# Five query buffers, three value buffers asked for at a step's end, and the second batch's raw keys behind the queries in SP's queue

## The chip, the cores and the metric

The program runs on one core of a Trainium2 chip. Its time is the device time of one execution in microseconds (us). A profiled execution gives, beside its time, a trace of what each engine did: TensorE (PE: matrix products, transposes), VectorE (DVE), ScalarE (ACT), GpSimd (POOL), and SyncE (SP), which here issues nearly all DMA transfers. Each engine takes its instructions in a fixed order and stands still when the next one has to wait.

## What is computed

Attention that keeps the 32 largest scores of each row, over 8 batches, 8 heads, 576 positions and 64 values per head; its output, 512 values for each of 4608 tokens, goes through a gated network of width 1536.

```python
scores = scale * np.matmul(q, k.transpose(0, 1, 3, 2))
kth = np.partition(scores, -top_k, axis=-1)[..., -top_k:-top_k + 1]
scores = np.where(scores >= kth, scores, -1000000000.0)
attn = np.exp(scores - np.max(scores, axis=-1, keepdims=True))
attn = attn / (np.sum(attn, axis=-1, keepdims=True) + 1e-09)
x = np.matmul(attn, v)            # heads side by side: 4608 x 512
gate = 1.0 / (1.0 + np.exp(-(x @ w_gate)))
out = (gate * (x @ w_val)) @ w_out
```

## The kernel before

**Tiling.** Attention goes in steps. A step is one tile of queries (128 positions, the fifth tile of a batch 64) of one pair of heads; a batch has 5 tiles and 4 pairs, so 20 steps. The steps stand in groups: for batch 0 the tiles 0 to 1, 2 to 3 and 4; for each later batch two groups. Within a group the pairs run outside and the tiles inside. Group 3 is the first of batch 1, so `kraw_3_1_2` is the raw key of the second batch, pair 1, head 2, while `u_0_1_0` belongs to batch 0, tile 1, pair 0.

**One step.** TensorE forms the scores, ScalarE copies them to SBUF (`s`). VectorE finds the top values of eight segments and of what they leave (`cand`, `tops`, `leads`). GpSimd makes the exponent's bias `st` (L344), ScalarE the signs `under` (L348), GpSimd the product `u` (L354), ScalarE the exponentials `e` (L285), VectorE the threshold and the masked `e` (L364, L290). TensorE transposes `e` (L376), ScalarE copies that to `et`, and TensorE weighs the values `v` with it. The output is kept as two parts, `xh` and `xl`, whose sum is the value.

**Keys, queries and values.** Batch 0 takes its keys and queries as they are. From batch 1 on a raw key (`kraw`, 128 x 576) is loaded by SP (L190), copied by ScalarE into the rounded key `k` (L192), and GpSimd subtracts the copy from the raw key in two halves of 288 columns (L194), which leaves the remainder in the lower 64 rows. Raw queries (`qraw`) are treated in the same way. The raw keys of batch 1 have a pool of their own, `bkr`, of one buffer, since the larger pool of the later batches takes memory that the splitting of the weights still holds; queries `qh` have three buffers (`bq`), values two (`bv`).

**Weights.** In the head of the program 18 weight tiles are split: SP loads `wraw` (two buffers, two transfers each), ScalarE, VectorE and TensorE (three products into `wrest`) make a high and a low part `w_split` (L150 to L171), and SP writes it to DRAM (`ws`, L172). The first network units take some of them from SBUF; all later ones are loaded back by SP (`w`, L459, 1 MB each, four buffers).

**The gated network.** Each unit of tokens (three of 256, then of 384) is a list of tasks: `wide` (`pz`, L473 to L475: twelve products for each of two outputs), ScalarE, VectorE and GpSimd for the gate, and `narrow` (L494 to L496). Tasks are put among the steps by milestones.

**What sets the order.** The main loop calls for step n the loads of keys two steps ahead (`fetch`), the value load if step n is the last tile of its pair in its group (`get_values`, L570), the query loads four steps ahead (`ask`) and the scores two steps ahead (`begin`); then the selection of step n, the masking of step n-1, weight splits or network tasks, and transposes and weighing of step n-2. From the end of the splitting on, the three look one step further. These calls are not the order of execution: a scheduler takes the instructions with their dependences and buffers and sets a fixed order for each engine and for SP's queue. `tc.issue_after(x)` in the code makes the scheduler place an instruction behind x. A load into a buffer that is still read waits in SP's queue, and what stands behind it waits too.

Of the kernel before, what the change touches and what calls it, by code (L numbers as in the profile page):

```python
# [30 lines left out]
def tile_topk_attention_then_gated_ffn(  # L31
# [10 lines left out]
    nc = tc.nc  # L42
# [33 lines left out]
    bi = ctx.enter_context(tc.tile_pool(name="bi", bufs=3))  # L76
    b2 = ctx.enter_context(tc.tile_pool(name="b2", bufs=2))
    bk = ctx.enter_context(tc.tile_pool(name="bk", bufs=2 * NP))
    bv = ctx.enter_context(tc.tile_pool(name="bv", bufs=2))
    b1 = ctx.enter_context(tc.tile_pool(name="b1", bufs=1))  # L80
    bs = ctx.enter_context(tc.tile_pool(name="bs", bufs=4))
    bq = ctx.enter_context(tc.tile_pool(name="bq", bufs=3))
    bqr = ctx.enter_context(tc.tile_pool(name="bqr", bufs=2))
    bkr = ctx.enter_context(tc.tile_pool(name="bkr", bufs=1))
    bx = ctx.enter_context(tc.tile_pool(name="bx", bufs=2 * NP))
    b3 = ctx.enter_context(tc.tile_pool(name="b3", bufs=3))
    dram = ctx.enter_context(tc.tile_pool(name="dram", bufs=1, space=bass.MemoryType.DRAM))
# [18 lines left out]

    w_split = [dram.tile([P, 2, 2, NP * P], F32, tag=f"ws{i}", name=f"ws{i}") for i in range(n_w)]

    pools, fresh, copies, ahead = {"first": bkr}, {}, [], []

    def ffn_pools():
        for name, bufs in (("w", 4), ("f2", 3), ("f4", NE), ("fg", FG + 1)):
# [68 lines left out]
    def load_keys(b, p, nm, plain):  # L181

        if plain:
            kt = bk.tile([P, S], F32R, tag="k", name=f"k_{nm}").bitcast(F32)
            (nc.sync if p else nc.scalar).dma_start(kt, k1[p])
            return [kt]
        ks = []
        for h in (2 * p, 2 * p + 1):
            raw = pools["kraw" if b > 1 else "first"].tile([P, S], F32, tag="kraw", name=f"kraw_{nm}_{h}")
            nc.sync.dma_start(raw, k[b, h])  # L190
            kt = bk.tile([P, S], F32R, tag="k", name=f"k_{nm}_{h}")
            nc.scalar.activation(kt, raw, AF.Copy)  # L192
            for part in (slice(0, HALF), slice(HALF, S)):
                nc.gpsimd.tensor_tensor(kt[D:, part], raw[D:, part], kt[D:, part], op=ALU.subtract)  # L194
            ks.append(kt)
        return ks

    def load_values(b, p, nm):
        vt = bv.tile([P, 11, D], F32, tag="v", name=f"v_{nm}")
        nc.sync.dma_start(vt, v[b, p].rearrange("p (c d) -> p c d", d=D))  # L200
        return vt

    def load_queries(b, i, p, plain):
        if plain:
            qt = bq.tile([P, 2 * P], F32R, tag="qh", name=f"qh_{b}_{i}_{p}").bitcast(F32)[:, :P]
            nc.sync.dma_start(qt, q1[i, p])
            return (qt,)
        raw = bqr.tile([P, 2 * P], F32, tag="qraw", name=f"qraw_{b}_{i}_{p}")
        nc.sync.dma_start(raw, q[b, i, p])
        qh, ql = [x.tile([P, 2 * P], F32R, tag=t, name=f"{t}_{b}_{i}_{p}") for x, t in ((bq, "qh"), (pools["ql"], "ql"))]  # L210
        nc.scalar.activation(qh, raw, AF.Copy)
        nc.gpsimd.tensor_tensor(ql, raw, qh, op=ALU.subtract)
        return qh, ql
# [301 lines left out]
    def run(general):  # L515
        steps = [(g, p, i) for g, (_, first, end) in enumerate(groups) for p in range(NP) for i in range(first, end)]
# [3 lines left out]
        def fetch(m):  # L520
            if m < len(steps) and steps[m][2] == groups[steps[m][0]][1]:
                g, p, _ = steps[m]
                b, first, _ = groups[g]
                if first == 0:
                    keys[b, p] = load_keys(b, p, f"{mark}{g}_{p}", not b and not general)

        def get_values(m):
            if steps[m][2] == groups[steps[m][0]][2] - 1:
                g, p, _ = steps[m]
                values[g, p] = load_values(groups[g][0], p, f"{mark}{g}_{p}")  # L530

        def begin(m):
            if m < len(steps):
                g, p, i = steps[m]
                staged[m] = scores(qs.pop(m), keys[groups[g][0], p], i, f"{mark}{groups[g][0]}_{i}_{p}")

        def ask(m):
            if m < len(steps):
                g, p, i = steps[m]
                qs[m] = load_queries(groups[g][0], i, p, not groups[g][0] and not general)  # L540
# [14 lines left out]
        fetched, asked, begun = FETCH, ASK, AHEAD  # L555
# [5 lines left out]
        for n in range(len(steps) + 2):  # L561
            if n < len(steps):
                g, p, i = steps[n]
                b, first, end = groups[g]
                m = n
                further = 1 if "spare" in pools else 0
                for m in range(fetched, n + FETCH + further + 1):
                    fetch(m)
                fetched = n + FETCH + further + 1
                get_values(n)  # L570
                for m in range(asked, n + ASK + further + 1):
                    ask(m)
                asked = n + ASK + further + 1
                for m in range(begun, n + AHEAD + further + 1):
                    begin(m)
                begun = n + AHEAD + further + 1
                J = 2 if i < NT else 1
                nm = f"{mark}{b}_{i}_{p}"
                if general:
                    parts[n] = select_any(J, staged.pop(n), nm)  # L580
                else:
                    parts[n] = select(J, staged.pop(n), col, nm)
                next(parts[n])
                col += J
# [18 lines left out]
            else:  # L603
# [5 lines left out]
                while todo and work < goal:  # L609
                    work += todo.pop(0)()  # L610
            if n < 2:
                continue
            g, p, i = steps[n - 2]
            b, first, end = groups[g]
# [24 lines left out]
            if p == NP - 1 and i == end - 1:  # L639
                while ready < len(units) and sum(units[ready]) <= b * S + min(end * P, S):  # L640
                    tasks = ffn(f"{mark}{ready}", [xs[ready, d] for d in range(NP)], *units[ready], orders[ready > 0], ready > 0)
                    kept = todo[-NE:] if ready > 1 and len(todo) >= NE else []
                    todo[len(todo) - len(kept) :] = tasks[: len(kept) > 0] + kept
                    todo += tasks[len(kept) > 0 :]
                    ready += 1
        for task in todo:
            task()

    run(False)


# [14 lines left out]
    with tc.If(again > 0):  # L666
        run(True)
# [54 lines left out]
```

## Time and profile before

| | |
|---|---|
| median of 3 runs | 1572.98 us (1570.57 to 1573.68) |
| profiled execution | 1572.65 us |
| its span in the trace | 1570.8 us |
| TensorE busy | 1515.2 us, 96% of the span |
| VectorE, ScalarE, GpSimd busy | 1286.7, 1115.9, 1067.2 us (82, 71, 68%) |
| moved by DMA | 344.14 MB, 219 GB/s on average |

The span runs from the first to the last record of the trace; the execution's own time is 1.85 us longer. The share of an engine is an average over stages: a row of forty equal slices shows where in the span an engine is idle. For a stretch of interest the trace can be asked for each engine's busy time, and for the instructions of one engine in order of time, each with the idle time ahead of it and what ended that. In such a row "x2" means that two instructions of the kind followed one another, and the duration is that of both.

### The profile page before, as it was taken

Reading aid. Unit: us, or ns where it says so; the run is one execution under the profiler, and the core shown is the slowest. Engines: PE = TensorE matmul, PEld = TensorE weight load, DVE = VectorE, ACT = ScalarE, POOL = GpSimd, SP = SyncE. Lnnn points to the kernel's source line nnn. Section 1 sums busy time; section 2 is a strip of 40 time slices with the busy share of each in tenths; the row PEclk is TensorE's granted clock in tenths of the full one; section 3 lists DMA queues with packets and bytes.
Section 4 is the critical chain, followed back from the end, with each engine's and each line's share of the span. In section 5 each row is a group of like instructions: output and inputs, shape, how many; then the busy total and the mean of one; then the engine's idle time right before and its main releaser. Section 6 shows DMA issues by size and latency. Waiting matters only on the chain. (4 is left out here: it accounts for less than half of the span.)

```text
span 1570.8 us, 33848 instructions
## 1 busy us (share of the span) xinstructions
PE 1515.2 (96%) x10586; PEld 1382.7 (88%) x10586; DVE 1286.7 (82%) x5806; ACT 1115.9 (71%) x2405; POOL 1067.2 (68%) x1756
## 2 busy tenths in 40 slices
PE   5779899999999999999999999999999999999998
PEld 2347689999999999899999999999999999999998
DVE  7899959999988789888988888987898888888311
ACT  8899867778776677786777667777777777667221
POOL 4566847798766877687666876687766886676211
PEclk9889999999999999999999999999999999999999
DMA  7664588787655765556655666565565575564574
GB/s 250 228 244 146 204 324 306 278 288 278 230 208 177 246 219 199 200 207 216 209 199 180 218 232 217 178 235 202 200 217 184 198 244 195 189 213 176 195 275 159
DMA packets 88894, 344.14 MB, mean 219 GB/s; under 512 B 9856, under 2 KB 36992, under 8 KB 57984
## 3 DMA queue, kind: packets, MB, share of 16 engines
q1 hardware_dynamic: 88560, 341.58, 62.5%
q8 instruction: 86, 1.41, 0.4%
q14 instruction: 104, 0.85, 0.2%
q10 hardware_dynamic: 144, 0.29, 0.1%
HBM read 313.52 MB, written 28.31 MB: 218 GB/s over the span
## 5 line engine op out<-in xcount | busy, mean ns | idle before, releaser
L354 POOL TENSOR_TENSOR u<-s,under 128x288 f32<-128x288 f32 x576 | 458.5, 818 | 141.7 <-ACT under L348 130.7
L336 DVE MAX8 cand<-s 128x8 f32<-128x72 f32 x2304 | 345.8, 217 | 66.6 <-ACT s L244 56.1
L473 PE MATMUL pz<-xh,w 128*128 128x384 f32 (+1 forms) x1184 | 391.4, 333 | 1.0 <-DVE acc L500 1.0
L475 PE MATMUL pz<-xh,w 128*128 128x384 f32 (+1 forms) x1184 | 391.3, 331 | 0.0
L474 PE MATMUL pz<-xl,w 128*128 128x384 f32 (+1 forms) x1184 | 390.2, 330 | 0.3 <-POOL xl L446 0.3
L290 DVE SCALAR_TENSOR_TENSOR e<-s,kths,e 128x576 f32<-128x576 f32 x288 | 281.9, 981 | 0.6 <-ACT e L285 0.3
L348 ACT ACTIVATE under<-s,leads 128x576 bf16<-128x576 f32 x288 | 223.0, 776 | 79.9 <-DVE leads L340 34.4
L364 DVE MAX8 kths<-u 128x8 f32<-128x584 f32 x288 | 219.3, 761 | 46.3 <-POOL u L355 44.6
L285 ACT ACTIVATE e<-s,st 128x576 f32<-128x576 f32 x288 | 209.8, 773 | 63.5 <-POOL st L344 62.9
L481 POOL TENSOR_TENSOR gl<-gf,gh 128x384 fp32r<-128x384 f32 (+1 forms) x156 | 153.7, 986 | 113.4 <-ACT gh L480 109.6
L473 PEld LDWEIGHTS pz<-xh,w 128*128 128x128 f32 x1184 | 223.1, 189 | 2.0 <-DVE acc L500 1.3
L474 PEld LDWEIGHTS pz<-xl,w 128*128 128x128 f32 x1184 | 223.5, 189 | 0.8 <-POOL xl L446 0.6
L475 PEld LDWEIGHTS pz<-xh,w 128*128 128x128 f32 x1184 | 223.4, 189 | 0.1
L377 ACT ACTIVATE et<-pt 128x384 f32<-128x384 f32 x384 | 178.6, 488 | 36.8 <-PE pt L376 35.1
L494 PE MATMUL po<-gh,w 128*128 128x384 f32 (+1 forms) x592 | 195.1, 334 | 1.7 <-DVE acc L500 1.6
L495 PE MATMUL po<-gl,w 128*128 128x384 f32 (+1 forms) x592 | 195.5, 331 | 0.5 <-POOL gl L481 0.5
L496 PE MATMUL po<-gh,w 128*128 128x384 f32 (+1 forms) x592 | 194.8, 330 | 0.0
L376 PE MATMUL pt<-ident,e 128*128 128x128 f32 x1152 | 180.8, 275 | 12.6 <-DVE e L290 9.2
L244 ACT ACTIVATE s<-pss 128x576 f32<-128x576 f32 x252 | 161.0, 639 | 40.3 <-PE pss L237 39.8
L376 PEld LDWEIGHTS pt<-ident,e 128*128 128x128 f32 x1152 | 141.0, 141 | 31.3 <-DVE e L290 9.2
L237 PE MATMUL pss<-k,qh 128*128 128x288 f32 (+2 forms) x588 | 165.2, 299 | 0.7 <-ACT s L244 0.7
L237 PE MATMUL pss<-k,ql 128*128 128x288 f32 (+2 forms) x588 | 160.3, 295 | 0.0
(108 smaller groups left out, 2911.1 us busy)
## 6 DMA issues: line engine op xcount, KB each, us to landing
w<-ws SPq DMA_DIRECT2D x222, 1024.0 KB, 5.0
v<-in_v_dram SPq DMA_DIRECT2D x68, 352.0 KB, 3.3
wraw<-in_w_dram SPq DMA_DIRECT2D x36, 512.0 KB, 4.9
ws<-w_split SPq DMA_DIRECT2D x18, 1024.0 KB, 4.5
qraw<-in_q_dram SPq DMA_DIRECT2D x140, 128.0 KB, 2.9
kraw<-in_k_dram SPq DMA_DIRECT2D x56, 288.0 KB, 3.6
out_dram<-acc SPq DMA_DIRECT2D x40, 192.0 KB, 4.7
out_dram<-acc SPq DMA_DIRECT2D x12, 128.0 KB, 6.5
```

The source lines that it names most:

```text
L237: nc.tensor.matmul(ps[:, half, o : o + n], x[:, h * P : (h + 1) * P], ks[h][:, k0 : k0 + n], start=t == 0, stop=t == len(todo) - 1,)
L285: nc.scalar.activation(e[:, j], s[:, j], AF.Exp, bias=st[:, j : j + 1], scale=1.0 / SHRINK)
L290: nc.vector.scalar_tensor_tensor(e[:, j], s[:, j], kth[j], e[:, j], op0=ALU.is_ge, op1=ALU.mult, accum_out=st[:, 4 + j : 5 + j])
L336: nc.vector.max(cand[:, j, 8 * g : 8 * g + 8], s[:, j, g * SEG : (g + 1) * SEG])
L348: nc.scalar.activation(under[:, j], s[:, j], AF.Sign, bias=bound, scale=-CUT, accum_out=sums[:, j : j + 1])
L354: nc.gpsimd.tensor_tensor(u[:, j, part], s[:, j, part], under[:, j, part], op=ALU.mult)
L364: nc.vector.max(kths[:, n_tiles - col - j : n_tiles - col - j + 8], u[:, j])
L376: nc.tensor.transpose(pt[:, c], ef[:, k0 : k0 + P], ident)
L473: nc.tensor.matmul(ps, wt[:, u, 0, d], xh, start=d == 0, stop=False)
L474: nc.tensor.matmul(ps, wt[:, u, 0, d], xl, start=False, stop=False)
L475: nc.tensor.matmul(ps, wt[:, u, 1, d], xh, start=False, stop=d == NP - 1)
L495: nc.tensor.matmul(ps, wt[:, e % 2, 0, f], gl, start=False, stop=False)
```

## The change

Three pools get more buffers: values 2 to 3, queries 3 to 5, raw keys of batch 1 from 1 to 2. Each query load is entered in a list, `requests`. A raw-key load of batch 1 must stand in SP's queue behind the query load that was entered last when `load_keys` ran. And `get_values(n)`, which stood ahead of the query loads of step n, is called when step n's other work has been written down.

```diff
--- before.py
+++ after.py
@@ -76,12 +76,12 @@
     bi = ctx.enter_context(tc.tile_pool(name="bi", bufs=3))
     b2 = ctx.enter_context(tc.tile_pool(name="b2", bufs=2))
     bk = ctx.enter_context(tc.tile_pool(name="bk", bufs=2 * NP))
-    bv = ctx.enter_context(tc.tile_pool(name="bv", bufs=2))
+    bv = ctx.enter_context(tc.tile_pool(name="bv", bufs=3))
     b1 = ctx.enter_context(tc.tile_pool(name="b1", bufs=1))
     bs = ctx.enter_context(tc.tile_pool(name="bs", bufs=4))
-    bq = ctx.enter_context(tc.tile_pool(name="bq", bufs=3))
+    bq = ctx.enter_context(tc.tile_pool(name="bq", bufs=5))
     bqr = ctx.enter_context(tc.tile_pool(name="bqr", bufs=2))
-    bkr = ctx.enter_context(tc.tile_pool(name="bkr", bufs=1))
+    bkr = ctx.enter_context(tc.tile_pool(name="bkr", bufs=2))
     bx = ctx.enter_context(tc.tile_pool(name="bx", bufs=2 * NP))
     b3 = ctx.enter_context(tc.tile_pool(name="b3", bufs=3))
     dram = ctx.enter_context(tc.tile_pool(name="dram", bufs=1, space=bass.MemoryType.DRAM))
@@ -106,7 +106,7 @@
     w_split = [dram.tile([P, 2, 2, NP * P], F32, tag=f"ws{i}", name=f"ws{i}") for i in range(n_w)]
-    pools, fresh, copies, ahead = {"first": bkr}, {}, [], []
+    pools, fresh, copies, ahead, requests = {"first": bkr}, {}, [], [], []
     def ffn_pools():
         for name, bufs in (("w", 4), ("f2", 3), ("f4", NE), ("fg", FG + 1)):
@@ -185,9 +185,11 @@
             (nc.sync if p else nc.scalar).dma_start(kt, k1[p])
             return [kt]
         ks = []
+        asked = requests[-1].ins
         for h in (2 * p, 2 * p + 1):
             raw = pools["kraw" if b > 1 else "first"].tile([P, S], F32, tag="kraw", name=f"kraw_{nm}_{h}")
-            nc.sync.dma_start(raw, k[b, h])
+            with tc.issue_after(asked) if b == 1 else ExitStack():
+                nc.sync.dma_start(raw, k[b, h])
             kt = bk.tile([P, S], F32R, tag="k", name=f"k_{nm}_{h}")
             nc.scalar.activation(kt, raw, AF.Copy)
             for part in (slice(0, HALF), slice(HALF, S)):
@@ -203,10 +205,10 @@
     def load_queries(b, i, p, plain):
         if plain:
             qt = bq.tile([P, 2 * P], F32R, tag="qh", name=f"qh_{b}_{i}_{p}").bitcast(F32)[:, :P]
-            nc.sync.dma_start(qt, q1[i, p])
+            requests.append(nc.sync.dma_start(qt, q1[i, p]))
             return (qt,)
         raw = bqr.tile([P, 2 * P], F32, tag="qraw", name=f"qraw_{b}_{i}_{p}")
-        nc.sync.dma_start(raw, q[b, i, p])
+        requests.append(nc.sync.dma_start(raw, q[b, i, p]))
         qh, ql = [x.tile([P, 2 * P], F32R, tag=t, name=f"{t}_{b}_{i}_{p}") for x, t in ((bq, "qh"), (pools["ql"], "ql"))]
         nc.scalar.activation(qh, raw, AF.Copy)
         nc.gpsimd.tensor_tensor(ql, raw, qh, op=ALU.subtract)
@@ -567,7 +569,6 @@
                 for m in range(fetched, n + FETCH + further + 1):
                     fetch(m)
                 fetched = n + FETCH + further + 1
-                get_values(n)
                 for m in range(asked, n + ASK + further + 1):
                     ask(m)
                 asked = n + ASK + further + 1
@@ -609,6 +610,7 @@
                 while todo and work < goal:
                     work += todo.pop(0)()
             if n < 2:
+                get_values(n)
                 continue
             g, p, i = steps[n - 2]
             b, first, end = groups[g]
@@ -643,6 +645,8 @@
                     todo[len(todo) - len(kept) :] = tasks[: len(kept) > 0] + kept
                     todo += tasks[len(kept) > 0 :]
                     ready += 1
+            if n < len(steps):
+                get_values(n)
         for task in todo:
             task()
```

The scheduler makes of it another order on SP and GpSimd, and, where keys are converted, on ScalarE. Three places show it. Names end in a running number; `<-` stands ahead of what is read.

**First place: SP's queue in the first part of the splitting**, where weights 3, 12 and 13 are loaded (`wraw`) and the split tiles written (`ws`). Before:

```order
L190 DMA kraw_3_0_1_2651<-in_k_dram 128x576
L206 DMA qh_0_1_2_282<-in_q1_dram 128x128
L135 DMA wraw_3_452<-in_w_dram 128x1024 x2
L190 DMA kraw_3_1_2_2828<-in_k_dram 128x576
L206 DMA qh_0_0_3_378<-in_q1_dram 128x128
L172 DMA ws1_124<-w_split_1_344 128x2048
L190 DMA kraw_3_1_3_2834<-in_k_dram 128x576
L135 DMA wraw_12_555<-in_w_dram 128x1024 x2
L172 DMA ws2_125<-w_split_2_364 128x2048
L206 DMA qh_0_1_3_481<-in_q1_dram 128x128
L135 DMA wraw_13_676<-in_w_dram 128x1024 x2
L190 DMA kraw_3_2_4_3093<-in_k_dram 128x576
```

After:

```order
L192 DMA kraw_3_0_0_2645<-in_k_dram 128x576
L192 DMA kraw_3_0_1_2651<-in_k_dram 128x576
L208 DMA qh_0_0_3_378<-in_q1_dram 128x128
L135 DMA wraw_2_363<-in_w_dram 128x1024 x2
L172 DMA ws0_123<-w_split_0_260 128x2048
L208 DMA qh_0_1_3_479<-in_q1_dram 128x128
L135 DMA wraw_3_452<-in_w_dram 128x1024 x2
L172 DMA ws1_124<-w_split_1_342 128x2048
L135 DMA wraw_12_553<-in_w_dram 128x1024 x2
L208 DMA qh_0_2_0_613<-in_q1_dram 128x128
L172 DMA ws2_125<-w_split_2_362 128x2048
L135 DMA wraw_13_676<-in_w_dram 128x1024 x2
```

Two raw keys now stand together ahead of weight 2, behind raw queries of batch 1, and the keys `kraw_3_1_2`, `kraw_3_1_3` and `kraw_3_2_4` have left the places between weights 3, 12 and 13; the queries `qh` stand further ahead.

**Second place: SP's queue at the end of the splitting**, from the last split tile that is written (`ws17`) through the first reloads of split weights (`w`). Before:

```order
L172 DMA ws17_140<-w_split_17_2261 128x2048
L209 DMA qraw_1_0_1_2659<-in_q_dram 128x256
L209 DMA qraw_1_1_1_2746<-in_q_dram 128x256
L459 DMA w_0_3_2417<-ws3_126 128x2048
L459 DMA w_0_12_2452<-ws12_135 128x2048
L459 DMA w_0_13_2484<-ws13_136 128x2048
L459 DMA w_1_0_2893<-ws0_123 128x2048
L200 DMA v_2_1_2657<-in_v_dram 128x704
L209 DMA qraw_1_0_2_2842<-in_q_dram 128x256
L209 DMA qraw_1_1_2_2959<-in_q_dram 128x256
L459 DMA w_1_1_3027<-ws1_124 128x2048
```

After:

```order
L172 DMA ws17_140<-w_split_17_2259 128x2048
L211 DMA qraw_1_0_1_2657<-in_q_dram 128x256
L211 DMA qraw_1_1_1_2744<-in_q_dram 128x256
L192 DMA kraw_3_1_2_2828<-in_k_dram 128x576
L192 DMA kraw_3_1_3_2834<-in_k_dram 128x576
L461 DMA w_0_3_2415<-ws3_126 128x2048
L461 DMA w_0_12_2450<-ws12_135 128x2048
L461 DMA w_0_13_2482<-ws13_136 128x2048
L461 DMA w_1_0_2891<-ws0_123 128x2048
L202 DMA v_2_2_2826<-in_v_dram 128x704
L211 DMA qraw_1_0_2_2840<-in_q_dram 128x256
L211 DMA qraw_1_1_2_2959<-in_q_dram 128x256
```

The four raw keys from `kraw_3_2_4` on, which stood before `ws17`, and the two of pair 1 are now behind the raw queries of batch 1: two here, ahead of the reload `w_0_3`, the other four behind the twelve rows shown.

**Third place: GpSimd's order around the second tile's `u`** (`u_0_1_0`), at the start of batch 0. Before:

```order
L355 TENSOR_TENSOR u_0_0_0_222<-wanted_110,sums_0_0_0_220 128x2x8
L194 TENSOR_TENSOR k_3_0_0_2647<-kraw_3_0_0_2645,k_3_0_0_2647 64x288 x2
L344 TENSOR_SCALAR st_0_1_0_295<-tops_0_1_0_294 128x2
L354 TENSOR_TENSOR u_0_1_0_298<-s_0_1_0_195,under_0_1_0_299 128x288 x2
L293 TENSOR_SCALAR st_0_0_0_219<-st_0_0_0_219 128x2
L354 TENSOR_TENSOR u_0_1_0_298<-s_0_1_0_195,under_0_1_0_299 128x288 x2
L355 TENSOR_TENSOR u_0_1_0_298<-wanted_110,sums_0_1_0_296 128x2x8
L296 COPY inv_0_0_0_342<-st_0_0_0_219 128x128
L194 TENSOR_TENSOR k_3_0_1_2653<-kraw_3_0_1_2651,k_3_0_1_2653 64x288 x2
L344 TENSOR_SCALAR st_0_0_1_391<-tops_0_0_1_390 128x2
L293 TENSOR_SCALAR st_0_1_0_295<-st_0_1_0_295 128x2
L194 TENSOR_TENSOR k_3_1_2_2830<-kraw_3_1_2_2828,k_3_1_2_2830 64x288 x2
```

After:

```order
L357 TENSOR_TENSOR u_0_0_0_222<-wanted_110,sums_0_0_0_220 128x2x8
L346 TENSOR_SCALAR st_0_1_0_293<-tops_0_1_0_292 128x2
L196 TENSOR_TENSOR k_3_0_0_2647<-kraw_3_0_0_2645,k_3_0_0_2647 64x288 x2
L196 TENSOR_TENSOR k_3_0_1_2653<-kraw_3_0_1_2651,k_3_0_1_2653 64x288 x2
L356 TENSOR_TENSOR u_0_1_0_296<-s_0_1_0_195,under_0_1_0_297 128x288 x2
L295 TENSOR_SCALAR st_0_0_0_219<-st_0_0_0_219 128x2
L298 COPY inv_0_0_0_340<-st_0_0_0_219 128x128
L356 TENSOR_TENSOR u_0_1_0_296<-s_0_1_0_195,under_0_1_0_297 128x288 x2
L357 TENSOR_TENSOR u_0_1_0_296<-wanted_110,sums_0_1_0_294 128x2x8
L346 TENSOR_SCALAR st_0_0_1_391<-tops_0_0_1_390 128x2
L295 TENSOR_SCALAR st_0_1_0_293<-st_0_1_0_293 128x2
```

The halves of the second key, `k_3_0_1`, have moved ahead of both parts of `u_0_1_0`; those of `k_3_1_2` have left this place.

## Rows read from the trace of the kernel before

**Rows 1.** The page: engines' busy time (share, instructions); TensorE's tenths in forty slices.

```profile
PE 1515.2 (96%) x10586; PEld 1382.7 (88%) x10586; DVE 1286.7 (82%) x5806; ACT 1115.9 (71%) x2405; POOL 1067.2 (68%) x1756
...
PE   5779899999999999999999999999999999999998
```

**Rows 2.** Windows: stretch, length, engines' busy us (instructions), granted clock, DMA share, GB/s.

```profile
0.00:40.00 40.00, 23.99 (x86) 11.75 (x88) 30.69 (x135) 32.36 (x52) 19.32 (x38) 0.95 0.71 245
40.00:80.00 40.00, 28.38 (x123) 14.66 (x119) 34.26 (x142) 33.86 (x59) 21.08 (x31) 0.84 0.69 237
80.00:120.00 40.00, 30.78 (x140) 17.11 (x139) 37.96 (x149) 36.70 (x66) 25.50 (x33) 0.83 0.69 243
160.00:200.00 40.00, 35.08 (x199) 25.12 (x199) 36.42 (x121) 35.44 (x70) 34.04 (x46) 0.91 0.61 206
230.00:240.00 10.00, 10.00 (x98) 9.80 (x97) 7.92 (x44) 7.59 (x17) 5.42 (x11) 1.00 0.99 402
```

**Rows 3.** Timeline of SP: start, us, line, transfer [idle before <-what ended it].

```profile
32.18 0.33 SPq L190 DMA_DIRECT2D kraw<-in_k_dram  x1
...
40.19 0.33 SPq L190 DMA_DIRECT2D kraw<-in_k_dram  x1
40.57 1.54 SPq L135 DMA_DIRECT2D wraw<-in_w_dram  x2
```

**Rows 4.** Timeline of GpSimd around 40 us.

```profile
36.76 3.40 POOL L194 TENSOR_TENSOR k<-kraw,k 64x288 fp32r<-64x288 f32 x2 [0.94 <-POOL st L293]
...
41.05 0.22 POOL L344 TENSOR_SCALAR st<-tops 128x2 f32<-128x2 f32 x1
```

**Rows 5.** Timeline of VectorE: the frac of a weight.

```profile
36.53 1.20 DVE L162 SCALAR_TENSOR_TENSOR wt_frac<-wraw 128x1024 fp32r<-128x1024 uint32 x1
```

**Rows 6.** Timeline of ScalarE ahead of the first hole.

```profile
41.30 1.44 ACT L285 ACTIVATE e<-s,st 128x576 f32<-128x576 f32 x2 [0.98 <-POOL st L344]
...
43.13 0.68 ACT L192 ACTIVATE k<-kraw 128x576 fp32r<-128x576 f32 x1 [0.39 <-DMA kraw<-in_k_dram]
...
48.88 1.34 ACT L152 ACTIVATE minus_zero<-wraw 128x1024 f16<-128x1024 f32 x1 [2.07 <-DMA wraw<-in_w_dram]
```

**Rows 7.** Timeline of TensorE: the first hole, and the network's first matmul.

```profile
53.38 1.90 PE L376 MATMUL pt<-ident,e 128*128 128x128 f32 x6 [6.29 <-DVE e L290]
...
107.67 0.68 PE L473 MATMUL pz<-xh,w_split 128*128 128x256 f32 x1
```

**Rows 8.** Timeline of ScalarE ahead of the second hole.

```profile
186.88 0.78 ACT L348 ACTIVATE under<-s,leads 128x576 bf16<-128x576 f32 x1 [2.69 <-POOL u L354]
...
189.59 0.69 ACT L192 ACTIVATE k<-kraw 128x576 fp32r<-128x576 f32 x1
...
191.47 1.10 ACT L171 ACTIVATE w_split<-wrest 128x512 fp32r<-128x512 f32 x2
```

**Rows 9.** Timeline of GpSimd ahead of the second hole.

```profile
179.06 0.79 POOL L194 TENSOR_TENSOR k<-kraw,k 64x288 fp32r<-64x288 f32 x1
...
180.63 1.65 POOL L194 TENSOR_TENSOR k<-kraw,k 64x288 fp32r<-64x288 f32 x1
...
184.44 2.40 POOL L354 TENSOR_TENSOR u<-s,under 128x288 f32<-128x288 f32 x2
```

**Rows 10.** Timeline of TensorE: the second hole.

```profile
192.14 0.39 PE L475 MATMUL pz<-xh,w_split 128*128 128x256 f32 x1 [1.83 <-ACT w_split L171]
```

**Rows 11.** Timeline of SP at the end of the splitting.

```profile
214.32 0.93 SPq L209 DMA_DIRECT2D qraw<-in_q_dram  x2
220.93 0.33 SPq L459 DMA_DIRECT2D w<-ws  x1
```

**Rows 12.** DMA from 205 to 262: sum; then an issue, KB each, us to landing.

```profile
DMA packets 4848, 19.72 MB, mean 346 GB/s; under 512 B 534, under 2 KB 2040, under 8 KB 2920
...
w<-ws SPq DMA_DIRECT2D x14, 1024.0 KB, 7.8
```

**Rows 13.** Timeline of TensorE: the first use of a reloaded weight.

```profile
230.18 0.28 PE L473 MATMUL pz<-xh,w 128*128 128x256 f32 x1
```

## The prediction

> **What bounds the kernel now.** I read the page's engine lines first. TensorE is busy 96% of the span, and its row of forty slices is full from the sixth slice on [rows 1]: after some 240 us nothing that the change touches can shorten the program unless it takes work from TensorE, and the change takes none. So the question is where TensorE stands idle. The table by stage [rows 2] has it: of 40 us each, TensorE is idle 16.0, 11.6 and 9.2 us in the first three stretches and 4.9 us from 160 to 200. That is 41.8 of the 55.6 us that the span holds beyond TensorE's busy time. There the gated network has no input yet (its first matmul starts at 107.67 us [rows 7]), and TensorE does what attention and the splitting of the weights hand to it. ScalarE and VectorE are busy for 31 to 38 of 40 us there, so TensorE waits for them, and they now and then for a transfer or for GpSimd.
>
> Then I followed two of these holes back, each through the timelines of the engines that wait for one another.
>
> The first, before 53.38 us, leaves TensorE idle 6.29 us for e [rows 7]. ScalarE had sat idle just ahead of it: 0.98 us for st on GpSimd, 0.39 us for a raw key, and 2.07 us for raw weights [rows 6]. Those weights were asked for at 40.57 us [rows 3], though their buffer was free when VectorE ended the frac of the weight two places earlier, at 36.53 + 1.20 = 37.73 us [rows 5]. What stood ahead of them in SP's queue was the load of a raw key, which left at 40.19 us, since its only buffer was in use until GpSimd had subtracted the key before it (3.40 us from 36.76) [rows 3, 4]. The st that ScalarE waited for came behind the same subtraction, at 41.05 us [rows 4].
>
> The second is at 192.14 us: TensorE idle 1.83 us for the last copy of a split weight on ScalarE [rows 10]. ScalarE had waited 2.69 us for u on GpSimd, and copied a raw key (0.69 us) before the copies TensorE wanted [rows 8]. GpSimd had done two halves of a key (0.79 and 1.65 us) shortly before that u [rows 9].
>
> **The change part by part.** *Keys of the second batch.* Eight raw keys are loaded, copied by ScalarE and subtracted by GpSimd in two halves, as before. Two keep an early place. The other six, of which two were converted before 50 us and four between 160 and 191, now come behind query loads that SP issues after 214 us (the first two places in the section on the change). The first hole loses ScalarE's three waits, 0.98 + 0.39 + 2.07 = 3.44 us, and two copies of 0.68 us, one of them in [rows 6]: 4.8 us. Against it stands the order of GpSimd: the second early key is now subtracted right behind the first, and both ahead of u of the second tile (the third place). Such a half took 0.79 us at the least and a pair 3.40 us at the most [rows 4, 9]; I take 1.8, near the low end, since one of the two pairs stood ahead of that u before, too. Net -3.0 us; the ends are -4.8 and, if only GpSimd's delay counts, +3.4. What is gained here is kept: the last pair's attention output, on which the network's first unit waits, comes behind as many VectorE instructions as before, so the whole chain moves as one.
>
> In the second hole one copy (0.69) and the two halves (2.44) leave the way of ScalarE's copies: 3.1 us, more than TensorE's wait of 1.83. I take -1.8. The ends are nothing, if VectorE's share of that stage is what decides, and the stretch's whole idle time of 4.9 us with the half-speed matmuls around it: 35.08 us of busy time at a granted clock of 0.91 [rows 2] would be 31.9 at full clock, so 4.9 + 3.2 = 8.1.
>
> The conversions themselves are not gone. Six copies of 0.7 us and twelve halves of 0.8 to 1.7 us fall into 215 to 262 us, where TensorE has network work and waits for neither engine; priced at nothing, and if that cover is gone, at most 6 x 0.7 = 4.2 us on ScalarE. The six loads (6 x 288 KB = 1.77 MB) fall there too, and SP's queue holds the reloads of split weights behind them. The stretch from 205 to 262 already moves 346 GB/s on average [rows 12]: 1.77 MB are 5.1 us of it. SP is idle from the queries at 214.32 to the weights at 220.93 [rows 11], so the two key loads between them delay no issue. Their 0.59 MB (1.7 us at 346 GB/s) do lie ahead of that weight, which lands about 7.8 us after its issue, at 228.7, and is used at 230.18 [rows 11 to 13]: a margin of 1.5 us. Later weights stand behind key loads that wait for GpSimd. I take +0.8, near the low end because the margin nearly covers the first; ends 0 and +5.1.
>
> *Queries in five buffers, values in three, asked for at a step's end.* No wait of TensorE on a query, a value or a weight reload is in its list after the first keys, so a shorter stay of these loads in SP's queue gains nothing by itself: 0, with -1.5 and +1.0 as ends, since a value that waits for a free buffer holds the weights behind it and one that is asked for later lands later. *Start.* Two query loads go ahead of early weights; one issue takes 0.33 us (the key's row [rows 3]): +0.3.
>
> Sum: -3.0 - 1.8 + 0.8 + 0 + 0.3 = -3.7 us. The profiled execution took 1572.65 us (a span of 1570.8 and 1.85 around it), 0.33 less than the median of the runs, 1572.98. That gives 1568.9 against the one and **1569.3 us** against the other.
>
> **The rivals.** *A larger gain.* If VectorE, too, runs freer once GpSimd is rid of conversions in the busy stretches, both upper ends are reached: -4.8 - 8.1 = -12.9, about 1560; I let this case run from 1557 to 1566. For it: a half of a key took 0.79 us once and 1.65 us the next time [rows 9], so GpSimd and something else hold each other up there. Against it: VectorE is busy 36.4 of the 40 us from 160, with work of its own [rows 2]. The Trainium skill (SBUF — State Buffer, Who interferes with whom) says that a VectorE instruction with two inputs in SBUF and a GpSimd instruction that reads SBUF exclude each other; by that rule every half taken out of the stretch gives VectorE its time back, and the sum would tend to this case. The spread of the halves agrees with it, though no row here shows whom they waited for.
>
> *No change.* Waits are handed on: once the raw weights are there, ScalarE waits for VectorE's top values or TensorE's scores instead, and the network's first unit starts when it did. For it: VectorE is idle only 5.7 and 2.0 us in the stretches from 40 and from 80 [rows 2], and its work ahead of that unit is unchanged. Against it: those 5.7 us lie around the hole that the change closes. This gives 1573 (1570 to 1576). That SP's order is changed but its waits fall elsewhere is the same case.
>
> *Slower.* The stage from 205 to 262 us becomes bound by transfers: split weights land after TensorE is ready for them. It decides from the point where a weight lands more than 1.5 us later than now, and costs up to 5.1 us: 1578.1 with nothing gained earlier, and 1581.5 if the two early keys cost their 3.4 us on top. The case runs from 1576 to 1582. The Trainium skill (DMA: Bandwidth & Descriptors, Specifications) puts HBM's limit for a core near 358 GB/s. By that rule the stage has almost no room and the moved loads cost their full 5 us; the mean of 346 GB/s agrees, but 402 GB/s from 230 to 240 us do not [rows 2].
>
> **How the numbers follow.** The forecast (1566 to 1571) has 42%, of which 32 lie below the bound; the larger gain 17%, no change 22%, slower 19%. A measurement of this kernel can tell some 0.2%, 3.1 us, from no change: faster means below 1569.8, slower above 1576.1. So faster 0.49, same 0.10 + 0.22 = 0.32, slower 0.19. The range goes from 1560 to 1578; it leaves out some 6% in the larger gain and some 11% in the slower case.
>
> **What would show it.** If the steps hold, the profile of the changed kernel has no wait of ScalarE for raw weights near 49 us, TensorE's first network matmul starts some 3 us before 107.67, the stretch from 160 to 200 has under 3 us of TensorE idle, and no wait of TensorE on w appears between 215 and 262. An unchanged start of the network's first matmul would speak for no change; waits of TensorE on w or k after 215 us, or on e shortly after the two early keys, would make the prediction wrong. A gain that lies behind 260 us would be none that I have foreseen.

## The result: 1.2% slower, and the profile after

The changed kernel took 1591.66 us in the median of five runs (1587.1 to 1595.97), the kernel before 1572.98, which is a median of five runs too: a ratio of 1.0124 with an interval of 1.0110 to 1.0138. The forecast was 1569.3 us, the range 1560 to 1578. The profiled execution is the fastest of the five, 1587.1 us with a span of 1585.3; so the trace shows 14.5 of the 18.7 us.

The page of the changed kernel, first the engines' busy time, then TensorE's tenths:

```profile
PE 1529.4 (96%) x10586; PEld 1384.6 (87%) x10586; DVE 1285.4 (81%) x5806; ACT 1117.9 (71%) x2405; POOL 1062.7 (67%) x1756
...
PE   6779999999999999999999999999999999999998
```

Against [rows 1] TensorE's idle time is as it was, 1585.3 - 1529.4 = 55.9 us (55.6 before). Its busy time has grown by 14.2 us, for the same 10586 products. The end of a product is modelled and products overlap, so short pauses count as busy. To see them I went to the start of each product: the time to the next start, less the columns of the first at 2.4 GHz, the granted clock there being 1.00. Pauses of 0.1 us or more between 260 and 1500 us come to 90.1 us in the kernel before and 107.6 in the changed one. The difference, 17.5 us, is most of the loss of this stretch; the level itself says little, since some 600 of these pauses are a regular step of 0.10 us. Counted from 0.13 us on they are 40.6 and 56.8 us, nearly the same difference.

The same starts show where it arises: when had TensorE streamed so many per cent of its columns?

```
share of TensorE's columns     4%      8%     12%     24%     36%     48%     60%     72%     80%     88%    100%
before, us                  130.1   209.5   271.2   452.4   627.8   806.7   983.1  1161.7  1279.8  1396.7  1564.8
changed, difference          -3.6    -5.1    -4.2    -0.8    +0.6    +3.6    +7.7    +8.5   +12.0   +15.2   +14.6
```

The head gains 5 us. From some 250 us on the kernel loses nearly 20, in small parts along the whole stretch. The stretches of the head, columns as in [rows 2], the fifth new:

```profile
0.00:40.00 40.00, 25.59 (x82) 11.38 (x82) 32.16 (x134) 33.93 (x54) 20.90 (x39) 0.96 0.84 303
40.00:80.00 40.00, 30.39 (x129) 15.38 (x128) 38.83 (x157) 36.99 (x64) 20.82 (x30) 0.89 0.67 235
80.00:120.00 40.00, 31.60 (x165) 17.97 (x163) 40.00 (x160) 34.24 (x64) 26.34 (x35) 0.93 0.60 210
160.00:200.00 40.00, 38.46 (x253) 28.07 (x252) 34.17 (x120) 35.94 (x66) 22.66 (x35) 1.00 0.55 203
205.00:262.00 57.00, 56.07 (x488) 50.86 (x487) 41.39 (x205) 39.74 (x96) 42.52 (x75) 1.00 0.97 373
```

For the body, the list of waits says what is new. The first line is of the changed kernel, the second, for the same copy of a raw query, of the kernel before (us in all, times, longest):

```profile
ACT qh L213 <- DMA qraw<-in_q_dram: 97.3, 69, 4.8
```

```profile
ACT qh L211 <- PE pss L237: 28.3, 27, 2.2
```

With three query buffers ScalarE's copy of a raw query was held back until TensorE had used an older query; the raw query had by then lain in SBUF for 12.5 us (median). With five nothing holds it, and the scheduler sets it earlier (where its own model has the load landing, as it seems): on the chip the copy starts 0.02 us (median) behind the landing, and in 69 cases ScalarE stands still for it. One such case, from GpSimd through SP and ScalarE to TensorE (timelines of the changed kernel, start, us, instruction):

```profile
1388.43 0.73 POOL L214 TENSOR_TENSOR ql<-qraw,qh 128x256 fp32r<-128x256 f32 x1
...
1389.19 0.33 SPq L211 DMA_DIRECT2D qraw<-in_q_dram  x1
...
1391.30 0.42 ACT L213 ACTIVATE qh<-qraw 128x256 fp32r<-128x256 f32 x1 [1.47 <-DMA qraw<-in_q_dram]
...
1393.68 0.64 ACT L246 ACTIVATE s<-pss 128x576 f32<-128x576 f32 x1
...
1394.38 0.40 PE L239 MATMUL pss<-k,qh 128*128 128x288 f32 x1 [0.64 <-ACT s L246]
```

The loads themselves are short (the same kernel's view of the tile `qraw`):

```profile
DMA to landing us min/median/max: 1.9/2.3/10.9
```

In the case above GpSimd gives one of the two raw buffers free, SP asks for the next query at once, ScalarE waits 1.47 us for it. Everything behind it on ScalarE is late, also the copy of scores at 1393.68 that empties their PSUM tile; the pool has one tile, and TensorE stands 0.64 us before the next scores.

The scores are not the only products that wait longer. TensorE's largest waits in the changed kernel from 450 to 1450 us (us in all, times, longest):

```profile
PE pt L378 <- ACT et L379: 2.8, 3, 1.5
PE po L496 <- DVE acc L502: 2.7, 4, 1.0
PE pss L239 <- ACT s L246: 1.9, 4, 0.7
```

The transposes wait for the copy of an earlier transpose, the network's output products for VectorE; in the kernel before the same three come to 0.7, 0.6 and 0.2 us.

### The profile page after: what moved, and what is told of

The parts are those of the page before. It is cut to its first block, busy times and chain, and to the rows that moved or that the text cites. A ratio compares the mean times of both kernels' runs of the same rounds, so it can differ in the third digit from the quotient of the medians.

```text
span 1585.3 us, 33689 instructions
## 1 busy us (share of the span) xinstructions
PE 1529.4 (96%) x10586; PEld 1384.6 (87%) x10586; DVE 1285.4 (81%) x5806; ACT 1117.9 (71%) x2405; POOL 1062.7 (67%) x1756
## 4 chain that ended last, share of the span: by engine, by line
PE 55%; DVE 17%; POOL 12%; ACT 10%; issue 4%; DMA 3%; POOLq 0%; ACTq 0%; DVEq 0%; SPq 0%
PE pz L475 8%; PE pz L477 8%; PE pz L476 8%; POOL u L356 6%; PE pss L239 6%; PE po L414 5%; PE po L496 4%; DVE cand L338 4%; PE po L498 4%; PE po L497 4%; PE pt L378 4%; DVE e L292 4%; DVE kths L366 3%; ACT under L350 2%; DMA qraw<-in_q_dram 2%
## 5 line engine op out<-in xcount | busy, mean ns | idle before, releaser
L292 DVE SCALAR_TENSOR_TENSOR e<-s,kths,e 128x576 f32<-128x576 f32 x288 | 278.6, 970 | 0.4 <-ACT e L287 0.2
```

The costliest lines, as they stand in the source:

```text
L292: nc.vector.scalar_tensor_tensor(e[:, j], s[:, j], kth[j], e[:, j], op0=ALU.is_ge, op1=ALU.mult, accum_out=st[:, 4 + j : 5 + j])
```

## The experiments

The first theory (Q) was what these lines suggest: ScalarE's waits for raw queries cost the 18 us. Sixteen kernels were run, each beside the kernel before, to which the ratio is taken (its median in those sessions was 1572.1 to 1572.7 us). The table has all of them; "at 8%, 24%, 100%" is the difference to the kernel before, as above, in the profiled executions; "pauses" are TensorE's of 0.1 us or more between 260 and 1500 us; "copy" is the mean time from a score tile's last product to the start of ScalarE's copy of it, between 400 and 1420 us.

| run | kernel | median us | ratio to before | at 8, 24, 100% | pauses us | copy us |
|---|---|---|---|---|---|---|
| before | | 1572.98 | | 0 | 90.1 | 0.94 |
| changed | | 1591.66 | 1.0124 [1.0110, 1.0138] | -5.1, -0.8, +14.6 | 107.6 | 1.21 |
| e1 | changed, 3 query buffers | 1571.10 | 0.9988 [0.9979, 0.9997] | -3.8, -3.6, -1.2 | 90.5 | 0.85 |
| e2 | before, 5 query buffers | 1576.99 | 1.0034 [1.0022, 1.0047] | -2.8, +0.2, +2.9 | 95.3 | 1.22 |
| e3 | before, keys' part | 1564.17 | 0.9950 [0.9937, 0.9962] | -8.0, -8.6, -8.4 | 88.2 | 0.95 |
| e4 | before, values' part | 1587.77 | 1.0099 [1.0084, 1.0113] | +5.0, +4.1, +16.9 | 102.2 | 1.32 |
| e5 | before, 3 value buffers | 1583.74 | 1.0075 [1.0061, 1.0089] | +2.6, +1.9, +11.6 | 99.7 | 1.20 |
| e6 | before, 2 raw-key buffers | 1578.68 | 1.0041 [1.0027, 1.0055] | -2.2, -3.0, +6.1 | 98.9 | 1.17 |
| e7 | changed, query copies placed | 1569.80 | 0.9983 [0.9974, 0.9992] | -4.7, -3.4, -3.7 | 86.1 | 0.93 |
| e8 | changed, 4 raw-query buffers | 1562.84 | 0.9941 [0.9928, 0.9955] | -9.1, -10.1, -9.9 | 87.8 | 0.93 |
| e9 | e5, placed | 1575.23 | 1.0019 [1.0011, 1.0028] | +3.0, +2.8, +2.8 | 90.5 | 0.90 |
| e10 | e6, placed | 1570.80 | 0.9990 [0.9981, 0.9998] | +2.0, +1.8, +2.9 | 90.3 | 1.02 |
| e11 | e3, placed | 1562.94 | 0.9944 [0.9931, 0.9958] | -8.5, -7.8, -9.4 | 85.1 | 0.91 |
| e12 | e3, 5 query, 4 raw-query buffers | 1572.35 | 1.0001 [0.9992, 1.0010] | -9.8, -9.9, -0.9 | 96.3 | 0.97 |
| e13 | e2, placed | 1567.10 | 0.9967 [0.9955, 0.9979] | -4.6, -6.4, -8.2 | 85.9 | 0.90 |
| e14 | e12, placed | 1564.34 | 0.9948 [0.9936, 0.9959] | -9.2, -8.9, -7.5 | 87.9 | 0.88 |
| e15 | e8, placed | 1567.77 | 0.9975 [0.9966, 0.9983] | -9.5, -8.5, -3.0 | 92.9 | 0.92 |
| e16 | before, values asked for later | 1572.50 | 1.0000 [0.9991, 1.0009] | +0.1, +0.1, -0.2 | 89.9 | 0.91 |

The profiled execution of e10, 1575.55 us, was the slowest of its eleven; the median is 4.8 us lower, so its differences are too high by as much.

**One part alone, or one taken back (e1 to e4).** The edits are the lines of the change; e1 is

```diff
-    bq = ctx.enter_context(tc.tile_pool(name="bq", bufs=5))
+    bq = ctx.enter_context(tc.tile_pool(name="bq", bufs=3))
```

> The changed kernel with the query pool back at three buffers; keys and values stay as changed. Theory Q (with five buffers ScalarE's copy of a raw query is placed where the load has only just been asked for, so ScalarE stands still for the landing, 97.3 us in 69 waits, and the slower steps cost TensorE some 18 us from 300 us on, while the moved keys keep their gain of some 4 us in the head): no wait of ScalarE for raw queries above 10 us in all, and 1569 us (1566 to 1573). Rival V (the later value loads and their third buffer disturb SP's queue): still above 1583. Rival R (the order of before is a lucky one, and any other order of the same work costs about a per cent): 1580 to 1595.

> The kernel before with five query buffers and nothing else. Theory Q: ScalarE waits 80 to 110 us for raw queries, the loss of some 18 us appears whole and without the head's gain: 1590 us (1584 to 1597). Rival V: 1573, no such loss. Rival R: 1580 to 1595, but without a wait of ScalarE for raw queries to explain it.

> The kernel before with the keys' part alone: two buffers for the second batch's raw keys and their loads behind the query load asked for last. Theory Q: the gain of the head alone, 1569 us (1566 to 1571); TensorE has done 8% of its columns some 4 to 5 us earlier than in the kernel before, and the lead lasts to the end. Rival K (the moved keys hurt the stage from 205 to 262 us or later): above 1575. Rival R: 1580 to 1595.

> The kernel before with the values' part alone: three value buffers and the value loads asked for at a step's end. Theory Q: within 0.2% of the kernel before, 1573 us (1570 to 1576), no wait of ScalarE for raw queries. Rival V: 1583 to 1592. Rival R: 1580 to 1595.

e1 came as theory Q has it: without the five query buffers the loss is gone. e3 gave more than expected, 8.5 us, all of it by 210 us and kept to the end; from batch 3 on its order on TensorE is that of the kernel before. e2 and e4 speak against Q. With five query buffers alone ScalarE waits as long as in the changed kernel, and it costs 6 us from 8% on, not 18:

```profile
ACT qh L211 <- DMA qraw<-in_q_dram: 103.7, 67, 4.7
```

And the values' part alone, in which no copy waits for a raw query, costs 15 us. That is the size that two rivals had forecast: that asking for values later costs (V, which e5 and e16 rule out), and that any other order costs about one per cent (R, which e1 to e3 contradict). In the head the parts add up (-8.0 - 2.8 + 5.0 = -5.8, measured -5.1); in the body they do not: keys and values together (e1) lose 2.4 us from 24% on, values alone 12.8.

**Which of the value edits, and what does another buffer do that has nothing to do with values (e5, e6, e16)?** e5 has the third value buffer alone, e16 the later request alone, e6 only

```diff
-    bkr = ctx.enter_context(tc.tile_pool(name="bkr", bufs=1))
+    bkr = ctx.enter_context(tc.tile_pool(name="bkr", bufs=2))
```

a buffer that only the eight raw keys of batch 1 use, in the head. On TensorE the scheduler's order for e6 is that of e5, row for row, from the start of batch 2 over 7497 of its 10586 products. A second theory (S) was that this other order as such costs, by setting attention earlier among the network's products.

> The kernel before with a third value buffer and nothing else; value loads are asked for where they were. Theory S (the extra buffer lets the scheduler set another order of TensorE for the whole of the program: from batch 4 on scores and transposes stand 10 to 30 network matmuls earlier than before, and TensorE meets scores whose PSUM tile ScalarE has not copied out yet): as slow as both value edits together, 1587 us (1583 to 1591), TensorE losing some 5 us by 250 us and the rest bit by bit up to 1400. Rival V (asking for the values later is what costs, their loads or what stands behind them): 1573 (1570 to 1576).

> The kernel before with a second buffer for the raw keys of batch 1 and nothing else: no value, no query and no load asked for in another place. The scheduler gives TensorE the same order from batch 1 on as in the kernel with a third value buffer. Theory S: after 300 us it loses what that kernel loses, some 12 us, whatever the head does: 1580 to 1588, and at least 10 of 256 score groups start within 0.15 us of the copy they wait for (3 before). Rival V or Q (values or queries themselves cost): no loss after 300 us, 1566 to 1574.

> The kernel before with its value loads asked for at a step's end, as in the changed kernel, but still two value buffers. The scheduler leaves 99% of each engine's rows where they were. All theories but V: 1572.5 us (1570 to 1575). Rival V (asking later costs by itself): above 1578.

Asking for values later costs nothing (e16, 99% of the rows unmoved). The third buffer does, and so does a second raw-key buffer: from 24% on e5 loses 9.7 us and e6 9.1. They lose it at the same places. The worst pause of either, ScalarE and TensorE, first e5, then e6, 4.9 us apart:

```profile
662.19 1.44 ACT L285 ACTIVATE e<-s,st 128x576 f32<-128x576 f32 x2 [1.86 <-POOL st L344]
663.54 0.67 ACT L192 ACTIVATE k<-kraw 128x576 fp32r<-128x576 f32 x1
664.11 0.40 ACT L211 ACTIVATE qh<-qraw 128x256 fp32r<-128x256 f32 x1
664.42 0.63 ACT L244 ACTIVATE s<-pss 128x576 f32<-128x576 f32 x1
...
665.10 0.40 PE L237 MATMUL pss<-k,qh 128*128 128x288 f32 x1 [1.33 <-ACT s L244]
```

```profile
657.29 1.45 ACT L285 ACTIVATE e<-s,st 128x576 f32<-128x576 f32 x2 [1.86 <-POOL st L344]
658.64 0.66 ACT L192 ACTIVATE k<-kraw 128x576 fp32r<-128x576 f32 x1
659.21 0.40 ACT L211 ACTIVATE qh<-qraw 128x256 fp32r<-128x256 f32 x1
659.51 0.63 ACT L244 ACTIVATE s<-pss 128x576 f32<-128x576 f32 x1
...
660.19 0.40 PE L237 MATMUL pss<-k,qh 128*128 128x288 f32 x1 [1.30 <-ACT s L244]
```

So the loss belongs to the order, not to values or their transfers. e6's median, 1578.68 us, lies between its two forecasts; its body lost 9.1 us where theory S had some 12. The rows also show what in the order may cost: a key copy and a query copy stand on ScalarE ahead of the copy that empties the scores' PSUM tile, and TensorE waits for that one. Here the query copy doesn't wait for a load; it stands in front. But it takes 0.3 us of TensorE's 1.33, and the first row has ScalarE idle for 1.86 us, waiting for st on GpSimd; what the query copies cost in all, these rows don't tell. In the slow bodies the score copy starts 1.17 to 1.32 us after the scores, in the kernel before 0.94; of some 200 score copies, those that began over 1.5 us after their scores and right behind a query copy are 25 in the kernel before, 37 and 36 in e5 and e6 (11 in the changed kernel, where the query copy stands further ahead and waits).

**Placing the query copy (e7), and asking for queries sooner (e8).** In e7 the copy is put behind the copy of the scores that were asked for last, where three buffers had held it; the fallback pass at the program's end is left as it was (the line that enters "general" in `pools` there is not shown):

```diff
-        nc.scalar.activation(qh, raw, AF.Copy)
+        with ExitStack() if "general" in pools else tc.issue_after(copies[-1].ins):
+            nc.scalar.activation(qh, raw, AF.Copy)
```

e8 has `bqr` with 4 buffers in place of 2.

> The changed kernel, five query buffers and all, with ScalarE's copy of a raw query put behind the copy of the scores asked for last, where three buffers had held it. Theory Q (ScalarE's wait for raw queries is what costs): the wait falls from 97 to under 10 us and the time to 1571 (1567 to 1575). Theory S (the order of TensorE costs: scores stand 15 to 100 network matmuls earlier than before here): the wait is gone, and the time stays at 1583 to 1595.

> The changed kernel with four buffers for raw queries in place of two, so that a query is asked for two steps earlier. In the scheduler's order for it TensorE's scores of batches 4 to 7 stand where they stood before (shift within 6 network matmuls). Theory S: 1570 us (1564 to 1575), though ScalarE still copies a query as soon as the model thinks it has landed. Theory Q: ScalarE still waits over 60 us for raw queries, and the time stays above 1583; or the wait is gone and it is 1571, in which case this run does not tell the two apart.

e7 ends theory S in its simple form: its scores stand 15 to 100 network products earlier than in the kernel before, and its body loses nothing. ScalarE's list of waits has no raw query any more, and for the score copies, which now come first:

```profile
ACT s L247 <- PE pss L240: 55.6, 59, 3.4
```

21.9 us come back by one placing. e8 does without it: queries land in time (no wait of ScalarE for one), the head gains 9 us, the body loses nothing. It came out below both forecasts for it, so it doesn't tell the theories apart. It is 0.59% faster than the kernel before, and one of the two fastest here.

**Does the placing take the loss away elsewhere (e9 to e15)?** The third theory (P): what costs in the body is query copies that stand or wait on ScalarE ahead of the score copy. All of these carry e7's edit, but e12. The rival (O) is that another order of the whole program costs, wherever the query copies stand; the placing changes the order, too.

> The kernel before with a third value buffer, and ScalarE's copy of a raw query put behind the copy of the scores asked for last. Theory P (the loss after 300 us comes from ScalarE's copies of raw queries that stand, or wait, ahead of the copy that empties the scores' only PSUM tile; the mean time from a score tile's last product to that copy was 0.94 us in the kernel before and 1.20 with the third buffer): that time falls under 1.0 us, the 9.7 us lost after 24% of TensorE's work are gone, and 1574 us (1570 to 1577) remain. Theory O (another order of the whole program costs, wherever the copies stand): still above 1580.

> The kernel before with a second raw-key buffer and the same placing of the query copies. Theory P: the 9.1 us lost after 24% of TensorE's work are gone and the head's gain of 3 us stays: 1569 us (1565 to 1573), with under 1.0 us from a score tile's last product to its copy. Theory O: above 1575.

> The keys' part alone, with the same placing of the query copies. Theory P: its body has no loss to give back, so it stays at 1564 us (1560 to 1567). Theory O: the order is new again, and anything from 1562 to 1582 may come.

> Keys' part, five query buffers and four buffers for raw queries, without the values' part: what the changed kernel with four raw buffers (1562.8 us) is worth without its third value buffer and later value loads. Theory P: no wait of ScalarE for raw queries above 10 us in all, and 1562 us (1558 to 1567). Theory O: 1562 to 1582.

> The kernel before with five query buffers (1577 us as such, ScalarE waiting 104 us for raw queries), and ScalarE's copy of a raw query put behind the copy of the scores asked for last. Theory P (query copies ahead of the score copies cost): the wait is under 10 us, the 6 us lost in the body are gone, the head's 3 us stay: 1570 us (1567 to 1573). Theory O (another order costs, wherever the copies stand): above 1575.

> Keys' part, five query buffers, four raw-query buffers (1572.4 us as such: 10 us gained in the head, 9 lost between 36 and 90% of TensorE's work) with the same placing. Theory P for this loss too: 1563 us (1560 to 1567). If this loss is of another kind: above 1569.

> The changed kernel with four raw-query buffers (1562.8 us as such) and the same placing. Theory P: little left to gain, 1562 us (1559 to 1566). Theory O: a new order, anything from 1560 to 1580.

The placing gave back 8.5 us with the third value buffer (e5 to e9), 7.9 with the second raw-key buffer (e6 to e10), 9.9 with five query buffers (e2 to e13), 8.0 in e14, and left e3 as it was (e11, 1.2 us less). In each of these the pauses of the body return to 85 to 91 us. Two runs do not fit. e12 loses 9 us in its body although ScalarE waits for no raw query and the score copies are hardly late (0.97 us). Among TensorE's waits there from 260 to 1500 us are 3.0 us for GpSimd's `xl` (0.3 in the kernel before) and 2.8 for the score copy (0.5); with the placing (e14) the first is gone and 2.5 us of the second stay. Why the order of e12 has them is open. And e15, e8 with the placing, is 4.9 us slower than e8: another order, with pauses of 92.9 us, and 3.9 us of waits for score copies although no query copy stands right ahead of a late one.

Theory P names the score copy as the way by which TensorE loses. The pauses, sorted by the product that they stand before, bear that out in part only (the first row in us, the others the difference to it, rounded):

| pauses before | scores | transposes | weighing | network | sum |
|---|---|---|---|---|---|
| before | 6.0 | 4.4 | 65.7 | 14.1 | 90.1 |
| changed | +4.9 | +3.9 | +4.6 | +4.0 | +17.5 |
| e7, changed and placed | +1.7 | -1.7 | -2.0 | -2.0 | -4.0 |
| e5, 3 value buffers | +5.3 | -0.3 | +1.9 | +2.6 | +9.6 |
| e9, e5 placed | +3.8 | +0.5 | -0.9 | -3.1 | +0.4 |

Before scores stand 4.9 of the 17.5 us in the changed kernel and over half in e5. From e5 to e9 only 1.5 us come back there, and 5.7 before the network's products. So these runs show that the place of the query copies is the large term: in all five kernels that lost in the body and were placed (changed, e2, e5, e6, e12), the loss went with the placing. They do not show that the score copy is the main way by which it reaches TensorE; a late ScalarE meets transposes, weighing and network, too. Some 5 us either way remain (e15) that the runs tie to the order and to nothing narrower.

## Why the prediction was wrong

**The head was right in its places; its size came in part by luck.** Forecast was -3.7 us by 262 us; the lead was 5.1 us at 8% and 4.2 at 12%. But the keys' part alone leads by 8.0 us at 8% (e3), where -3.0 - 1.8 = -4.8 was forecast up to there; the queries' part adds 2.8 of gain (e2), the values' part 5.0 of loss (e4), and both had been put at nothing, but for 0.3 at the start. The sum agrees in part because these errors offset one another. Why the values' part costs 5 us in the head, no run shows. ScalarE's wait for raw weights ahead of the first hole [rows 6] is gone, the transposes come without idle time, and of its three waits the one for st remains, as the price put on GpSimd's order had it. Of the changed kernel, ScalarE and TensorE:

```profile
42.50 1.44 ACT L287 ACTIVATE e<-s,st 128x576 f32<-128x576 f32 x2 [1.06 <-POOL st L346]
...
49.17 1.37 ACT L152 ACTIVATE minus_zero<-wraw 128x1024 f16<-128x1024 f32 x1
...
53.08 0.49 PE L378 MATMUL pt<-ident,e 128*128 128x128 f32 x3
...
100.32 1.20 PE L475 MATMUL pz<-xh,w_split 128*128 128x256 f32 x1
```

The network's first product starts 7.4 us earlier, where 3 were forecast; at 4% of the columns 3.6 us of it are left. The second hole is closed: from 160 to 200 us TensorE is idle 1.5 us (under 3 forecast) at a granted clock of 1.00, against 4.9 and 0.91 [rows 2].

**The moved loads cost nothing that lasts.** The price of 0.8 us and the slower rival rested on a stage without room at 346 GB/s [rows 12]. The changed kernel moves more there, and TensorE's list of waits from 205 to 262 us holds no weight. About 1 us of the lead is gone between 8 and 12% in the changed kernel and in e3 alike (e3: 8.0, then 7.0), but at 24% e3 leads by 8.6. The DMA view of that stretch, the changed kernel, then e3:

```profile
DMA packets 5824, 21.28 MB, mean 373 GB/s; under 512 B 653, under 2 KB 2189, under 8 KB 3971
```

```profile
DMA packets 5846, 22.05 MB, mean 387 GB/s; under 512 B 653, under 2 KB 2189, under 8 KB 3861
```

The Trainium skill (DMA: Bandwidth & Descriptors, Specifications) has a core's share of HBM near 358 GB/s; 387 over 57 us is above it, and the measurement decides. The six copies of keys on ScalarE fell between 223 and 261 us, as forecast, GpSimd's halves between 224 and 265, and TensorE waits for none of them.

**The step that failed** is the term for queries and values: "0, with -1.5 and +1.0 as ends", since no wait of TensorE on a query, a value or a weight reload was in its list. It measured +5.7 us for queries alone and +11.9 for values alone from 8% to the end, and 19.7 for all parts together. Three things were wrong in it. It asked only what the loads do in SP's queue, and looked only at TensorE's waits; the copies of the queries are ScalarE's, one engine further back. It doesn't speak of the wait for a buffer of queries that stood in ScalarE's list, 28.3 us in 27 cases; that wait was what kept the copy behind the score copy and behind the landing. And it took the body for settled, because TensorE is full there: "after some 240 us nothing that the change touches can shorten the program unless it takes work from TensorE". Full is not safe, since TensorE is full only as long as ScalarE's copies come in time, and an instruction of 0.4 us at another place, or a wait for a load, makes them late. Nor is full the end: with five query buffers and the placing (e13) the lead grows from 4.6 us at 8% to 8.2 at the end. For the query buffers the order was there to be read: between a query's copy and the first copy of its scores stand 33 instructions on ScalarE in the kernel before (median), 53 in the changed one. I had compared the orders at the head alone. For the third value buffer this number would not have told: it is 33 in e5 as well, and why one more buffer there gives this order is open.

**The rivals.** The slower side had 19%, with one mechanism, at 205 to 262 us, priced at 5.1 us, or 8.5 with the early keys; the direction came, but by another mechanism, at another place and price. So the range ended at 1578. The larger gain, put at about 1560 for a head that runs freer, is about what e8 and e11 reached (1562.8 and 1562.9 us) once the body was left in peace, though no run shows that it came by the port of SBUF that was named beside it.

## What to carry to other kernels

A further buffer is not only room: where a planner sets the order, a buffer wait is also what keeps an instruction in its place, and each pool's size is an input to the whole order. Before a buffer is added, compare the order of every engine over the whole program, and for the engine that must stay full ask which copy frees its next tile and what now stands ahead of it. A copy whose input comes by DMA belongs behind the work that others wait for: here the placing took the loss away in five kernels. It is no rule without exception; on top of four raw-query buffers it cost 5 us (e15), and those buffers without it (e8) were as fast as anything here.

## What the runs showed of the hardware

TensorE's idle time doesn't show short pauses: it was 55.6 and 55.9 us in two executions of which one holds 17.5 us more of pauses of 0.1 us or more; only the starts of the products tell. In the changed kernel a transfer of 128 KB landed in 2.3 us in the median (1.9 at the least), and a queue that asks for it only when its buffer comes free passes these 2 us on to whoever stands first in line. The 16 DMA engines kept 387 GB/s over 57 us in e3, where the 346 of the kernel before had been priced as a limit.
